# An instruction order from a time model of the engines, and 232 of 4096 exp blocks on VectorE, in a two-layer transformer kernel

## The chip, the cores and the metric

The kernel runs on one core of a Trainium2 chip. The core has TensorE (PE, matrix products into PSUM), ScalarE (ACT, functions of one element such as exp), VectorE (DVE, elementwise work), GpSimd (POOL) and SyncE (SP, which issues DMAs here). Each engine has a queue of its own instructions, in the order in which the program writes them, and waits on semaphores for the others. The metric is the device time of one execution in microseconds; the time given is the median of several runs.

## The reference

```
x = A_x                                     # (1, 2048, 512), bf16
x = x + attention(layernorm(x), wqkv, wo)   # 32 heads of 16 columns
x = x + relu(layernorm(x) @ w1) @ w2        # 512 -> 1792 -> 512
x = x + attention(layernorm(x), wqkv, wo)   # the same weights again
x = x + relu(layernorm(x) @ w1) @ w2

# attention: q, k, v = x @ wqkv, by head
scores = einsum("bhqd,bhkd->bhqk", q, k) * 16 ** -0.5
o      = einsum("bhqk,bhkd->bhqd", softmax(scores), v)
result = o @ wo
```

The scores are 2 layers x 32 heads x 2048 x 2048 numbers, and each goes through an exp.

## The kernel before, in words

Everything stays in SBUF: the weights, the rows `x`, the transposed keys `ktp`, and the values `vaug`, which carry a column of ones beside each head so that the product of probabilities and values also gives the sum of the row. The queries of a layer are cut into four chunks `j` of 512 columns (QS). A *block* is one head, one chunk of 512 queries and one tile of 128 keys (`kb`): one score matmul of 16 used rows (four heads lie in the four row groups of the array) into one PSUM bank of 128 x 512. There are 2 x 4 x 32 x 16 = 4096 blocks.

A *segment* is four heads over the 16 key tiles, 64 blocks. The heads of a group of eight are split in two sets of four by a mask on the queries (`mask[e]`, `qbuf`). Their four P·V products are accumulated in one PSUM bank `ps_o`, each in its own 32 partitions. In the first chunk of layer two, six segments are cut in two runs: the first takes the early key tiles and stores `ps_o` in `acc` ("store"), the second takes the last four key tiles and adds it ("load"), since the last keys of that layer come late.

The main loop takes three blocks (W) at a time, a *slot*. Per slot it writes the score matmuls into one of two PSUM tiles `ps_s` of three banks; then one exp on ScalarE over all 1536 columns into one of four `ebuf` (L628); then the P·V matmuls of the slot before (L545, `emit_pv`); then *pieces* of other work. These pieces are pairs of matmuls of 512 columns, or four transposes, into the one bank `ps_f`: q of the next run, keys, values, output projection, and the two dense products. All of it stands in the lists `urgent` and `work`, and VectorE's part (evacuations of `ps_f`, layer norms, the division by the row sums) in `evac` and `dve_q`. What comes next was chosen by counts of slots: `mark` notes the slot in which a result was written, `ready` asks that it be of an earlier slot, `pace` says how many matmuls of pieces a slot takes, `run_dve(900)` how much of VectorE's list, and `level` counts matmuls. Where `level` falls under FLOOR = 3.4 per slot, the scores are written two or three times (`times`), which changes no result and keeps TensorE occupied.

At the end of a segment (`finish_segment`) VectorE copies `ps_o` to `u`; only then may the next segment's P·V write the bank. Three small DMAs bring the row sums into `c`, bring their reciprocals back to `u`, and spread them over `r`; then VectorE multiplies `u` by `r` into `ot`. After the last segment of a chunk, `rest_of_chunk` puts the projection, layer norms and dense products of that chunk into the list, and they are worked off as pieces of the next chunk.

Of the kernel before, what the change touches and what calls it, by code (L numbers as in the profile page):

```python
# [9 lines left out]
FP32 = mybir.dt.float32  # L10
# [10 lines left out]
def kernel(  # L21
# [34 lines left out]
    FLOOR = 3.4  # L56
# [9 lines left out]
    mask = [sb([P, 1], FP32, f"mask{e}") for e in range(2)]  # L66
    wqkv = sb([P, NDC, 3 * D], BF16, "wqkv")
# [22 lines left out]
    acc = [sb([P, QS], FP32, f"acc{t}") for t in range(NACC)]  # L90
# [53 lines left out]
    slot = [0]  # L144
    made = {}

    def mark(key, lag=0):
        made[key] = slot[0] + lag

    def emitted(deps):  # L150
        return all(k in made for k in deps)

    def ready(deps):
        return all(k in made and (wide[0] or made[k] < slot[0]) for k in deps)
# [5 lines left out]
    dve_q = []  # L160

    def left():
        return sum(c for q in (urgent, work) for g in q for c, _ in g["pieces"]) + sum(
            c for c, _ in cur
        )

    def pick(test):
        for q in (urgent, work):
            for g in q:
                if test(g["deps"]):  # L170
                    q.remove(g)
                    cur.extend(g["pieces"])
                    return True
        return False

    owed = [0.0]

    def run_pe(budget):
        spent = 0.0
        owed[0] = min(owed[0] + budget, 2.0 + budget)  # L180
        while owed[0] > 0:
            if not cur:
                if evac or not pick(ready):
                    break
            c, fn = cur.popleft()
            fn()
            owed[0] -= c
            spent += c
        return spent

    def run_dve(budget):
        i = 0
        while i < len(dve_q) and budget > 0:
            c, deps, fn = dve_q[i]
            if ready(deps):
                dve_q.pop(i)
                fn()
                budget -= c
            else:
                i += 1  # L200

    def run_evac():
        while evac:
            evac.popleft()()

    def force():

        if evac:
            run_evac()
            return True  # L210
        if cur or pick(emitted):
            cur.popleft()[1]()
            return True
        for i, (c, deps, fn) in enumerate(dve_q):
            if emitted(deps):
# [465 lines left out]
```

## Time and profile before

| | |
|---|---|
| median of 3 runs | 2041.85 us (2036.95 to 2048.78) |
| the profiled execution's own time | 2039.66 us |
| its span, first to last instruction | 2037.9 us |
| its mean granted TensorE clock | 0.971 |
| ScalarE busy | 1871.7 us (92%) |
| TensorE busy (matmuls) | 1690.9 us (83%) |
| VectorE busy | 436.9 us (21%) |
| DMA, mean | 14 GB/s |

The profile is of one execution. In its list of groups a row gives line, engine, operation, what is written and read, the form (partitions x elements), how many, the busy time and mean length of one, and the idle time of the engine just before them with what ended it. In the timeline a row gives start and length in us, and in brackets the idle time before it. A busy TensorE is not one at its peak: matmuls overlap, and their ends are modelled. The granted clock is the share of full speed that TensorE's throttle let through.

### The profile page before, as it was taken

What the parts mean: (1) busy time and instruction counts of PE and PEld (TensorE: products, weight loads), DVE (VectorE), ACT (ScalarE), POOL (GpSimd) and SP (SyncE); (2) the same over time, 40 slices, a digit from 0 to 9 for tenths busy, and PEclk for the clock granted to TensorE, in tenths of its full rate; (3) what the DMA queues carried; (4) which work ended last, traced back from release to release, by engine and by line L of the source; (5) the groups of instructions that cost most, each with busy time, mean ns of one, the idle gap of its engine ahead of it and who ended that gap; (6) DMA issues with size and microseconds to landing.
All of it is one profiled execution on the core that took longest, in us unless ns stands there. A gap on an engine that the chain in (4) does not pass through costs nothing.

```text
span 2037.9 us, 30025 instructions
## 1 busy us (share of the span) xinstructions
PE 1690.9 (83%) x13604; PEld 523.4 (26%) x13604; DVE 436.9 (21%) x927; ACT 1871.7 (92%) x1407; POOL 2.4 (0%) x35
## 2 busy tenths in 40 slices
PE   5777778888888888888889877898888888888876
PEld 2222222222222222222222222222222222222222
DVE  5111102212132132212133220211112111121122
ACT  2799999999999999999989999999999999999960
POOL 0000000000000000000000000000000000000000
PEclk8999999999999999999899989989998999989998
DMA  4000000000000000000000010000000000000000
GB/s 155 1 12 12 12 7 12 12 12 6 12 12 11 7 12 12 10 8 12 12 1 1 4 30 9 9 12 12 17 12 12 10 12 19 12 9 10 17 11 11
DMA packets 34131, 29.42 MB, mean 14 GB/s; under 512 B 17492, under 2 KB 25428, under 8 KB 34004
## 3 DMA queue, kind: packets, MB, share of 16 engines
q1 hardware_dynamic: 32420, 25.94, 5.6%
q8 instruction: 106, 1.74, 0.3%
q10 hardware_dynamic: 1584, 1.57, 0.2%
q14 instruction: 21, 0.17, 0.0%
HBM read 7.86 MB, written 2.10 MB: 5 GB/s over the span
## 4 chain that ended last, share of the span: by engine, by line
ACT 71%; PE 17%; DVE 8%; DMA 3%; issue 1%; SPq 0%; DVEq 0%
ACT e L628 71%; PE ps_s L621 6%; PE ps_f L243 5%; PE ps_o L545 4%; DMA r<-u 2%; PE ps_s L243 2%; DVE u L494 1%; DVE ht L400 1%; DVE q L371 1%; PE ps_s L579 1%; DVE stats L260 1%; DMA u<-c 1%; PE ps_f L298 0%; DVE xn L288 0%; ACT xnT L573 0%
## 5 line engine op out<-in xcount | busy, mean ns | idle before, releaser
L628 ACT ACTIVATE e<-ps_s 128x1536 bf16<-128x1536 f32 x1366 | 1847.9, 1581 | 55.1 <-PE ps_s L621 54.2
L621 PE MATMUL ps_s<-q,ktp 32*128 32x512 bf16 x7704 | 812.2, 385 | 221.2 <-ACT e L628 218.8
L545 PE MATMUL ps_o<-e,vaug 128*32 128x512 bf16 x4096 | 568.7, 396 | 45.3 <-DVE u L494 34.6
L621 PEld LDWEIGHTS <-ktp 32*128 32x128 bf16 x7704 | 257.2, 92 | 714.5 <-issue 659.7
L545 PEld LDWEIGHTS <-vaug 128*32 128x32 bf16 x4096 | 138.1, 93 | 490.3 <-issue 490.3
L243 PE MATMUL ps_f<-xn2T,w 128*128 128x512 bf16 x400 | 121.2, 391 | 11.1 <-DVE q L371 5.1
L400 DVE TENSOR_SCALAR ht<-ps_f 128x512 bf16<-128x512 f32 x99 | 68.4, 691 | 281.0 <-PE ps_f L243 281.0
L243 PE MATMUL ps_f<-w,ht 128*128 128x512 bf16 x406 | 120.0, 383 | 1.0
L499 DVE SCALAR_TENSOR_TENSOR ot<-u,mask,r 128x512 bf16<-128x512 f32 (+1 forms) x67 | 48.7, 727 | 276.5 <-DMA r<-u 273.8
L494 DVE COPY u<-ps_o 128x512 f32<-128x512 f32 x58 | 40.1, 691 | 266.5 <-PE ps_o L545 266.5
L243 PE MATMUL ps_f<-xnT,wqkv 128*128 128x512 bf16 x248 | 74.1, 389 | 1.4 <-DVE vaug L363 0.2
L371 DVE TENSOR_SCALAR q<-ps_f,mask 128x512 bf16<-128x512 f32 x68 | 47.9, 746 | 90.2 <-PE ps_f L243 90.2
L243 PE MATMUL ps_f<-wo,ot 128*128 128x512 bf16 x224 | 66.2, 386 | 0.8
L414 DVE TENSOR_TENSOR x<-x,ps_f 128x512 bf16<-128x512 bf16 x29 | 20.0, 688 | 189.2 <-PE ps_f L243 189.2
L386 DVE TENSOR_TENSOR x<-x,ps_f 128x512 bf16<-128x512 bf16 x28 | 19.2, 687 | 161.1 <-PE ps_f L243 161.1
L243 PEld LDWEIGHTS <-w 128*128 128x128 bf16 x448 | 32.0, 99 | 76.4 <-issue 67.5
L260 DVE BATCH_NORM_STATS2 stats<-x 128x6 f32<-128x512 bf16 x64 | 44.0, 687 | 7.0 <-DMA x<-in_A_x_dram 5.6
L338 DVE CAST ktp<-ps_f 128x512 bf16<-128x512 f32 x28 | 19.4, 692 | 117.1 <-PE ps_f L243 117.1
L243 PEld LDWEIGHTS <-ht 128*128 128x128 bf16 x448 | 29.1, 97 | 57.5 <-issue 47.9
L398 ACT ACTIVATE ht<-ps_s 128x512 bf16<-128x512 f32 x6 | 3.6, 597 | 42.8 <-PE ps_s L243 42.8
L298 PE MATMUL ps_f<-ident,xn 128*128 128x128 bf16 x188 | 21.8, 249 | 16.3 <-DVE xn L288 10.0
L298 PEld LDWEIGHTS <-xn 128*128 128x128 bf16 x256 | 18.4, 109 | 54.6 <-DVE xn L288 31.7
(54 smaller groups left out, 303.1 us busy)
## 6 DMA issues: line engine op xcount, KB each, us to landing
r<-u SPq DMA_DIRECT2D x63, 256.0 KB
w<-in_B_w_dram SPq DMA_DIRECT2D x2, 1792.0 KB
x<-in_A_x_dram SPq DMA_DIRECT2D x16, 128.0 KB
out_dram<-x SPq DMA_DIRECT2D x16, 128.0 KB
wqkv<-in_A_wqkv_dram ACTq DMA_DIRECT2D x3, 512.0 KB
c<-u SPq DMA_DIRECT2D x63, 8.0 KB
u<-c SPq DMA_DIRECT2D x63, 8.0 KB
wo<-in_A_wo_dram SPq DMA_DIRECT2D x1, 512.0 KB
```

The lines of the kernel that those rows point to most:

```text
L243: nc.tensor.matmul(b, lhsT, rhs, start=(i == 0), stop=(i == n - 1))
L260: nc.vector.bn_stats(out=st[:], in_=x_t[j * TPC + i][:])
L298: nc.tensor.transpose(pt[:, c * P : (c + 1) * P], xnbuf[i][:, c * P : (c + 1) * P], ident[:])
L371: nc.vector.tensor_scalar(out=qbuf[n % 2][e][:], in0=b, scalar1=mask[e][:, 0:1], scalar2=None, op0=ALU.mult,)
L400: nc.vector.tensor_scalar(out=ht[ft][:], in0=b, scalar1=0.0, scalar2=None, op0=ALU.max)
L414: nc.vector.tensor_add(out=x_t[tt][:], in0=x_t[tt][:], in1=b)
L494: nc.vector.tensor_copy(out=u[:], in_=ps_o[:])
L499: nc.vector.scalar_tensor_tensor(out=ot[t][:, a : a + w], in0=u[:, a : a + w], scalar=mask[e][:, 0:1], in1=r[:, a : a + w], op0=ALU.mult, ...
L545: nc.tensor.matmul(ps_o[32 * g : 32 * g + 32, :], vaug[sg["l"]][kb][:, 4 * sg["T"] + g, 2 * e : 2 * e + 32], s["e"][:, w, :], start=(kb == ...
L579: nc.tensor.matmul(b, lhsT, rhs, start=(i == 0), stop=(i == len(mms) - 1))
L621: nc.tensor.matmul(b[:, w, :], kt[32 * g : 32 * g + 32, kc : kc + P], qbuf[sg["n"] % 2][sg["e"]][32 * g : 32 * g + 32, :], start=True, sto ...
L628: ex = nc.scalar.activation(out=eb[:, :m, :], in_=b[:, :m, :], func=ACTF.Exp, scale=SCALE)
```

## The change

**The order.** The counts of slots give way to clocks, kept while the program is written: `now_pe`, `now_dve` and `exp_end`, in nanoseconds, with a fixed cost for each task, for a hand-over between engines and for a switch of TensorE between kinds of work. `mark` notes an engine and a time, and `at` says when another engine may use the result. `fill_pe` writes pieces ahead of a slot's scores as far as they end before these are needed, `times` is limited by the room that is left, and the floor is 0.56 of the time. `run_dve` takes VectorE's work in three classes: `musts` (the copy of `ps_o`, the first step of a block's exp), then evacuations, then tasks. When a segment ends in a slot, the rest of that slot's P·V is written after the next slot's scores.

**The blocks.** In segments that neither store nor load, a slot may give its third block to VectorE: its exp then covers 1024 columns. Blocks come in pairs, two slots apart. `first_step` adds a bias to the scores, which the mask on the queries (now `qmask`) has scaled so that they read as exponent and fraction of a float, and writes them as whole numbers in `di`. For the two halves together `chain` takes out the fraction (`dm`), runs a cubic polynomial on it in three steps (`dy`, `dy`, `de`), and keeps the exponent in `di`. The probability is the sum of twice `de` and the upper half of `di`, and that sum is formed on TensorE: six P·V matmuls for a pair instead of two. A pair begins where no other is open, not later than the slot 12 of a segment, and where `now_dve` with the tasks that could run is less than 3000 ns ahead of `now_pe`. It comes out as two pairs in each of the 58 segments. `acc` now shares the space of `dm`, `dy` and `di`.

Matmuls in the program: scores 7704 before, 6503 after; P·V 4096 before, 3864 + 464 (`de`) + 232 (`di`) after. The order before the first exp and behind the last keeps its work.

VectorE where chunk 2 of layer two has just been projected, at the end of the first segment of chunk 3 (`ya` ends a layer norm's small operations, `xn` are its four normalizations, `ot` is the multiply by `r`, `q` are the two masked copies of the next queries, `u` is the copy of `ps_o`). Before:

```order
L282 SCALAR_TENSOR_TENSOR ya_199<-ta_201,ya_199 128x4
L499 SCALAR_TENSOR_TENSOR ot_161<-u_183,mask_64,r_185 128x512
L288 TENSOR_SCALAR xn_189<-x_78,mv_195,ya_199 128x512
L288 TENSOR_SCALAR xn_190<-x_79,mv_195,ya_199 128x512
L288 TENSOR_SCALAR xn_191<-x_80,mv_195,ya_199 128x512
L288 TENSOR_SCALAR xn_192<-x_81,mv_195,ya_199 128x512
L371 TENSOR_SCALAR q_0_181<-ps_f,mask_64 128x512
L371 TENSOR_SCALAR q_1_182<-ps_f,mask_65 128x512
L494 COPY u_184<-ps_o 128x512
L323 COPY xn2T<-ps_f 128x4x128 x2
```

The copy of `ps_o` stands behind the multiply, the normalizations and the queries. After:

```order
L386 SCALAR_TENSOR_TENSOR ya_199<-ta_201,ya_199 128x4
L617 COPY u_184<-ps_o 128x512
L707 TENSOR_SCALAR di<-ps_s_205 128x512
L732 TENSOR_SCALAR dm<-di 128x1024
L738 SCALAR_TENSOR_TENSOR dy<-dm 128x1024
L481 TENSOR_SCALAR q_0_181<-ps_f,qmask_66 128x512
L481 TENSOR_SCALAR q_1_182<-ps_f,qmask_67 128x512
L738 SCALAR_TENSOR_TENSOR dy<-dy,dm 128x1024
L738 SCALAR_TENSOR_TENSOR de<-dy,di 128x1024
L732 TENSOR_SCALAR di<-di 128x1024
L392 TENSOR_SCALAR xn_189<-x_80,mv_195,ya_199 128x512
```

The copy comes right behind the layer norm's small operations, then a first step; queries and normalizations stand within and behind the chain.

TensorE at the same segment end (`ps_s` scores, `ps_o<-e` P·V; `vaug_15` and `vaug_0` are the values of the last and the first key tile). Before:

```order
L621 LDWEIGHTS ktp_1_0_105
L621 MATMUL ps_s_204<-q_0_179,ktp_1_0_105 128x512
L545 LDWEIGHTS vaug_15_129
L545 MATMUL ps_o<-e_177,vaug_15_129 32x512
L545 LDWEIGHTS vaug_0_130
L545 MATMUL ps_o<-e_177,vaug_0_130 32x512 [waits DVE_49]
L545 LDWEIGHTS vaug_0_130
L545 MATMUL ps_o<-e_177,vaug_0_130 32x512
L621 LDWEIGHTS ktp_1_0_105
L621 MATMUL ps_s_205<-q_0_179,ktp_1_0_105 128x512 [waits Activation_49]
```

The P·V of the next segment, which waits for VectorE's copy, stands ahead of the scores of the next slot. After:

```order
L668 LDWEIGHTS vaug_15_131
L668 MATMUL ps_o<-e_177,vaug_15_131 32x512
L849 LDWEIGHTS ktp_1_0_107 [waits DVE_49]
L849 MATMUL ps_s_205<-q_0_179,ktp_1_0_107 128x512 [waits Activation_49]
L849 LDWEIGHTS ktp_1_0_107
L849 MATMUL ps_s_205<-q_0_179,ktp_1_0_107 128x512
L849 LDWEIGHTS ktp_1_0_107
L849 MATMUL ps_s_205<-q_0_179,ktp_1_0_107 128x512
L668 LDWEIGHTS vaug_0_132
L668 MATMUL ps_o<-e_177,vaug_0_132 32x512 [waits DVE_49]
```

The scores of the next slot stand ahead of that P·V; they wait for VectorE themselves, for the first step that reads the same tile.

A pair's six matmuls on TensorE, in the second segment of layer two's third chunk; before there are none:

```order
L668 LDWEIGHTS vaug_4_136
L668 MATMUL ps_o<-e_177,vaug_4_136 32x512
L668 LDWEIGHTS vaug_0_132
L668 MATMUL ps_o<-de,vaug_0_132 32x512 [waits DVE_49]
L668 LDWEIGHTS vaug_2_134
L668 MATMUL ps_o<-de,vaug_2_134 32x512
L668 LDWEIGHTS vaug_0_132
L668 MATMUL ps_o<-de,vaug_0_132 32x512
L668 LDWEIGHTS vaug_2_134
L668 MATMUL ps_o<-de,vaug_2_134 32x512
L668 LDWEIGHTS vaug_0_132
L668 MATMUL ps_o<-di,vaug_0_132 32x512 [waits DVE_49]
```

Both halves read `de` twice and the upper half of `di` once (two rows further, for the other half); the first matmul waits for the chain.

The diff, cut:

```
--- before.py
+++ after.py
...
-    FLOOR = 3.4
...
+    KAPPA_BITS = 0x00170000
+    LOG2E = 1.4426950408889634
+    UNIT = float(1 << 23)
+    EXP_BIAS = (126.0 + math.log2(2.0 * LEAD)) * UNIT
...
+    MM = 216.0
+    SWITCH = 105.0
+    PE_TO_DVE, DVE_TO_PE, ACT_TO_PE, PE_TO_ACT = 220.0, 100.0, 240.0, 222.0
+    FLOOR = 0.56
+    LAST_PAIR = 12
+    BACKLOG = 3000.0
...
+    dm = sb([P, 2, QS], FP32, "dm")
+    dy = sb([P, 2, QS], FP32, "dy")
+    di = sb([P, 2, QS], FP32, "di")
+    de = sb([P, 2, QS], BF16, "de")
+    acc = [x[:, k, :] for x in (dm, dy, di) for k in range(2)]
...
+    def at(keys, engine):
+
+        t = 0.0
+        for k in keys:
+            if k not in made:
+                return None
+            e, when = made[k]
+            if e != engine:
+                when += PE_TO_DVE if engine == "dve" else DVE_TO_PE
+            t = max(t, when)
+        return t
...
+    def pe_start(kind, ready=0.0):
+        return max(now_pe[0] + (SWITCH if mode[0] != kind else 0.0), ready)
+
+    def pe_run(kind, units, ready=0.0):
+        now_pe[0] = pe_start(kind, ready) + units * MM
+        mode[0] = kind
+        busy[0] += units * MM
...
+    def fill_pe(limit):
+
         while owed[0] > 0:
+            limit_now = limit if owed[0] < 5.0 else now_pe[0] + 1000.0
...
+                start = pe_start("f", bank_free[0] + DVE_TO_PE) + 50.0
+                for g in (g for q in (urgent, work) for g in q):
+                    t = at(g["deps"], "pe")
+                    if t is not None and t <= start:
+                        break
+                else:
+                    return
+                if start + g["pieces"][0][0] * MM > limit_now:
+                    return
+                start_group(g)
+            elif pe_start("f", cur[0][2]) + cur[0][0] * MM > limit_now:
+                return
+            do_piece()
...
+    def run_dve(until, musts):
+
+        while True:
+            can = [(0, m[1], m) for m in musts[:1]]
+            if now_dve[0] < until:
+                can += [(1, e[1], None) for e in list(evac)[:1]]
+                for t in dve_q:
+                    ready = at(t["deps"], "dve")
+                    if ready is not None:
+                        can.append((2, ready, t))
+            if not can:
+                return
+            soon = [c for c in can if c[1] <= now_dve[0] + 40.0]
+            kind, ready, x = min(soon, key=lambda c: c[0]) if soon else min(can, key=lambda c: c[1])
+            if kind and ready >= until:
+                if not musts:
+                    return
+                kind, ready, x = can[0]
+            if kind == 0:
+                musts.pop(0)
+                dve_run(x[0], x[1])
+                x[2]()
+            elif kind == 1:
+                do_evac()
             else:
-                i += 1
-
-    def run_evac():
+                do_task(x)
...
+        def masked(b, e):
+            nc.vector.tensor_scalar(
+                out=qbuf[n % 2][e][:], in0=b, scalar1=qmask[e][:, 0:1], scalar2=None,
+                op0=ALU.mult,
+            )
+
         def fin(b):
-            for e in range(2):
-                nc.vector.tensor_scalar(
-                    out=qbuf[n % 2][e][:], in0=b, scalar1=mask[e][:, 0:1], scalar2=None,
-                    op0=ALU.mult,
-                )
-            mark(("q", n))
+            masked(b, 0)
...
+        if n > 1:
+            run_until(("m", n - 2))
...
+                mark(("c", n), lag=2600.0)
...
+            mark(("r", n), lag=5500.0)
...
+    def dve_block(half, sg, kb, g, src, ex, recent):
+        def first_step():
+            first = nc.vector.tensor_scalar(
+                out=di[:, half, :].bitcast(I32), in0=src, scalar1=EXP_BIAS, scalar2=0.0,
+                op0=ALU.add, op1=ALU.max,
+            )
+            tc.declare_no_dep(
+                first.ins, ex.ins, reason="both only read the scores, and in different banks"
+            )
+            for earlier in recent:
+                tc.declare_no_dep(
+                    first.ins, earlier,
+                    reason="the scores read here were written after it, and are waited for",
+                )
+            step1_end[slot[0]] = now_dve[0]
+            if half == 1:
+                chain(pairs[-1]["key"])
+
+        if half == 0:
+            assert not pairs
+            pair_no[0] += 1
+            pairs.append({"sg": sg, "key": ("e", pair_no[0]), "blocks": []})
+        pairs[-1]["blocks"].append((kb, g))
+        musts.append((690, now_pe[0] + PE_TO_DVE, first_step))
...
+    def chain(key):
+        def bits(out, keep, put):
+            nc.vector.tensor_scalar(
+                out=out[:].bitcast(I32), in0=di[:].bitcast(I32), scalar1=keep,
+                scalar2=put, op0=ALU.bitwise_and, op1=ALU.bitwise_or,
+            )
+
+        def step(out, x, c, y):
+            nc.vector.scalar_tensor_tensor(
+                out=out[:], in0=x[:], scalar=c, in1=y[:], op0=ALU.add, op1=ALU.mult
+            )
+
+        steps = (
+            (690, lambda: bits(dm, 0x007FFFFF, 0x3E800000)),
+            (1260, lambda: step(dy, dm, C2, dm)),
+            (1260, lambda: step(dy, dy, C1, dm)),
+            (1260, lambda: step(de, dy, C0, di)),
+            (690, lambda: bits(di, 0x7F800000, KAPPA_BITS)),
+        )
+        for n, (cost, fn) in enumerate(steps):
+            k = key + (n,) if n + 1 < len(steps) else key
+            task(cost, fn, [k], [key + (n - 1,)] if n else [], place=n)
+
+    def emit_pair():
+        p = pairs.popleft()
+        pe_run("v", 3, at([p["key"]], "pe"))
+        halves = list(enumerate(p["blocks"]))
+        tops = di[:].bitcast(BF16)
+        for rhs in (de, de, None):
+            for half, (kb, g) in halves:
+                pv(p["sg"], kb, g, tops[:, half, 1::2] if rhs is None else rhs[:, half, :])
 
 
...
+        pace = 3.0 if sg["store"] or sg["load"] else max(todo / max(rest - 6.0, 6.0), 0.5)
+        owed[0] = min(owed[0] + pace, 6.0) if todo else 0.0
+        s_ready = max(exp_end[no - 2] + ACT_TO_PE, step1_end.get(no - 2, 0.0) + DVE_TO_PE)
+        need_by = exp_end[no - 1] - MM - PE_TO_ACT
+        fill_pe(max(need_by - 60.0, s_ready) - SWITCH)
+
...
+        spare = int(max(need_by - pe_start("s", s_ready), 0.0) / MM)
+        times = 1 + min(spare, 0 if level >= 0 else 1 if level > -MM else 2)
...
+        half = None
+        if len(now) == W and now[0][0] is sg and not (sg["load"] or sg["store"]):
+            r = (kb * 4 + g - 2) // W
+            if pair_at is not None:
+                half = 1 if r == pair_at + 2 else None
+            elif (
+                not pairs
+                and r <= LAST_PAIR
+                and now_dve[0] + sum(t["cost"] for t in dve_q if at(t["deps"], "dve") is not None)
+                < now_pe[0] + BACKLOG
+            ):
+                half = 0
+        if half is not None:
+            pair_at = r if half == 0 else None
+        m = len(now) - (half is not None)
+        ex = nc.scalar.activation(
+            out=eb[:, :m, :], in_=b[:, :m, :], func=ACTF.Exp,
+            scale=1.0 / (LOG2E * UNIT),
...
+        copies = len(musts)
+        while len(pend) > 1 and len(musts) == copies:
             emit_pv()
...
+            and (at([pairs[0]["key"]], "pe") or 1e18) <= now_pe[0] + 60.0
+            and all(x[0] is pairs[0]["sg"] for x in list(pend[0]["blocks"])[:1])
+        ):
+            emit_pair()
...
+        level = min(level + busy[0] - FLOOR * (exp_end[no] - exp_end[no - 1]), 90.0)
+        run_dve(exp_end[no - 1] + ACT_TO_PE, musts)
```

More of the change, by code (lines that the diff above doesn't have):

```diff
@@ L1 @@
+import math
 from contextlib import ExitStack
@@ L533, with pv @@
     pend = deque()
-    last_exp = [None] * NE
+    musts = []
+    exps = [deque(maxlen=6) for _ in range(NE)]
+    def pv(sg, kb, g, rhs, stop=False):
+        e = sg["e"]
+        nc.tensor.matmul(
+            ps_o[32 * g : 32 * g + 32, :],
+            vaug[sg["l"]][kb][:, 4 * sg["T"] + g, 2 * e : 2 * e + 32],
+            rhs, start=g not in sg["begun"], stop=stop,
+            tile_position=(0, 32 * g), skip_group_check=True,
+        )
+        sg["begun"].add(g)
     def emit_pv():
@@ L568 @@
                     op=ALU.add, axis=mybir.AxisListType.XY,
+                )
+            for e in range(2):
+                nc.vector.tensor_scalar(
+                    out=qmask[e][:], in0=mask[e][:], scalar1=SCALE * LOG2E * UNIT, scalar2=None,
+                    op0=ALU.mult,
                 )
```

290 lines of the change are left out of this document (174 added, 116 removed).

## The prediction

> **What bounds the kernel now.** I read the page first, its busy shares, the chain that ended last and the costliest groups:
>
> ```profile
> PE 1690.9 (83%) x13604; PEld 523.4 (26%) x13604; DVE 436.9 (21%) x927; ACT 1871.7 (92%) x1407; POOL 2.4 (0%) x35
> ...
> ACT 71%; PE 17%; DVE 8%; DMA 3%; issue 1%; SPq 0%; DVEq 0%
> ...
> L628 ACT ACTIVATE e<-ps_s 128x1536 bf16<-128x1536 f32 x1366 | 1847.9, 1581 | 55.1 <-PE ps_s L621 54.2
> L621 PE MATMUL ps_s<-q,ktp 32*128 32x512 bf16 x7704 | 812.2, 385 | 221.2 <-ACT e L628 218.8
> L545 PE MATMUL ps_o<-e,vaug 128*32 128x512 bf16 x4096 | 568.7, 396 | 45.3 <-DVE u L494 34.6
> ```
>
> ScalarE's exp (L628) is the limit: 1847.9 us of work, with only 55.1 us idle before it. The score matmuls wait 218.8 us for exp; exp waits 54.2 us for them. TensorE looks 83% busy, but the score row counts 7704 matmuls for 4096 blocks: the rest repeat scores to keep TensorE occupied. VectorE is idle four fifths of the time.
>
> Next, ScalarE's timeline, for the price of an exp, and the query on the exp's line:
>
> ```profile
> 128.49 86.24 ACT L628 ACTIVATE e<-ps_s 128x1536 bf16<-128x1536 f32 x64 [0.37 <-PE ps_s L621]
> ...
> 358.83 1.45 ACT L628 ACTIVATE e<-ps_s 128x1536 bf16<-128x1536 f32 x1 [0.60 <-PE ps_s L621]
> ...
> L628 ACT ACTIVATE e<-ps_s x1366: 602/1557/1802, 67.4 to 1969.8; 128x1536 bf16<-128x1536 f32 x195, 128x512 bf16<-128x512 f32 x1
> ```
>
> Alone, an exp of three blocks takes 1.45 us. In a train of 64 the pitch is (86.24 - 1.45) / 63 = 1.346 us, so two neighbours overlap by 0.104. The shortest, 602 ns, is the one exp of a single block that ends the queue of blocks. Exps run from 67.4 to 1970; what lies before and after (67 and 68 us) the diff leaves in its order.
>
> Third, the waits of ScalarE, for the whole run and for five stretches (67 to 965, 965 to 1207, and three of 17 to 20 us at 1320, 1555 and 1795):
>
> ```profile
> ACT e L628 <- PE ps_s L621: 54.2, 109, 2.4
> ...
> ACT e L628 <- PE ps_s L621: 13.8, 28, 1.3
> ...
> ACT e L628 <- PE ps_s L621: 23.0, 43, 2.1
> ...
> ACT e L628 <- PE ps_s L621: 2.7, 7, 0.6
> ...
> ACT e L628 <- PE ps_s L621: 4.0, 8, 1.5
> ...
> ACT e L628 <- PE ps_s L621: 4.3, 8, 2.4
> ```
>
> The 23.0 lie in the runs that store and load `acc`, where matmul pieces are pushed at pace 3.0; 11.0 in the three short stretches. The last of these, in the timeline and by windows:
>
> ```profile
> 1790.97 0.16 DVE L282 SCALAR_TENSOR_TENSOR ya<-ta,ya 128x4 f32<-128x4 f32 x1
> 1791.06 0.75 DVE L499 SCALAR_TENSOR_TENSOR ot<-u,mask,r 128x512 bf16<-128x512 f32 x1
> ...
> 1791.73 1.38 DVE L288 TENSOR_SCALAR xn<-x,mv,ya 128x512 bf16<-128x512 bf16 x4
> ...
> 1793.02 1.41 DVE L371 TENSOR_SCALAR q<-ps_f,mask 128x512 bf16<-128x512 f32 x2
> ...
> 1794.34 0.69 DVE L494 COPY u<-ps_o 128x512 f32<-128x512 f32 x1
> ...
> 1795.08 0.61 PE L545 MATMUL ps_o<-e,vaug 128*32 128x512 bf16 x2 [2.25 <-DVE u L494]
> ...
> 1797.14 1.45 ACT L628 ACTIVATE e<-ps_s 128x1536 bf16<-128x1536 f32 x1 [2.39 <-PE ps_s L621]
> ...
> 1809.18 18.91 ACT L628 ACTIVATE e<-ps_s 128x1536 bf16<-128x1536 f32 x14 [0.21 <-PE ps_s L621]
> ...
> 1797.00:1806.00 9.00, 9.00 (x58) 2.72 (x55) 1.86 (x5) 7.67 (x6) 0.00 (x0) 0.50 0.09 18
> ```
>
> At the end of a segment the copy of `ps_o` stands on VectorE behind a multiply, four normalizations and two q copies. TensorE, in order, waits 2.25 us for it, exp waits 2.39 us, and after this gap the granted clock (last but two columns of the window) is 0.50. Seven exps then take 12.04 us, 1.72 each.
>
> **The change, part by part.**
>
> *232 blocks leave ScalarE.* The order of the changed program holds 1366 exps still, 232 of them of 1024 columns. Between 0.602 for one block and 1.45 for three, a block costs 0.424 us, so an exp of two has a pitch of 0.922: 232 x 0.424 = 98 us less. At most it is a third of the pitch, 0.449 (104 us); at least 0.32 (74 us), if the shorter exp lost the overlap of 0.104. I take 98, since an exp of two lies between two measured sizes and stands in the same train.
>
> *VectorE takes them.* Rows for its durations:
>
> ```profile
> L494 DVE COPY u<-ps_o 128x512 f32<-128x512 f32 x58 | 40.1, 691 | 266.5 <-PE ps_o L545 266.5
> ...
> L499 DVE SCALAR_TENSOR_TENSOR ot<-u,mask,r x67: 352/752/754, 109.7 to 1977.3; 128x512 bf16<-128x512 f32 x63, 128x128 bf16<-128x128 f32 x4
> ...
> L278 DVE SCALAR_TENSOR_TENSOR ta<-ya 128x4 f32<-128x4 f32 x48 | 7.8, 162 | 1.6
> ```
>
> The first step (L707) reads one PSUM bank as the `u` copy does: 232 x 0.69 = 160 us. Three two-tensor steps per pair have 1024 columns: between 0.752 + 0.59 = 1.34 (752 less the 162 of a four-column one, once more) and twice 0.752; at 1.34 they are 348 x 1.34 = 466. The two steps on bits read SBUF alone, and no row has their form: four normalizations of 512 columns took 1.38, so 0.69 per 1024 at that rate, or 1.38 at the `u` copy's; 160 or 320 us. VectorE so goes from 437 to about 1220 us (at the upper ends 1440), 63% to 75% of 1930. It does not become the bound by sum. A pair's chain lasts 5.4 us (upper ends 7.3).
>
> *New wait: scores behind the first step.* Scores of exp n+2 overwrite the bank that the first step of exp n reads, and the order shows that wait on their first weight load, with everything on TensorE queued behind. Score rows and their waits:
>
> ```profile
> 200.00 0.61 PE L621 MATMUL ps_s<-q,ktp 32*128 32x512 bf16 x6 [0.19 <-ACT e L628]
> ...
> 700.13 0.39 PE L621 MATMUL ps_s<-q,ktp 32*128 32x512 bf16 x3
> ...
> 700.45 0.40 PE L545 MATMUL ps_o<-e,vaug 128*32 128x512 bf16 x3
> ...
> 701.31 0.10 PEld L621 LDWEIGHTS <-ktp 32*128 32x128 bf16 x3 [0.42 <-issue]
> ```
>
> Scores n end about 0.6 us after exp n-2 ends; exp n then ends 1.346 + 0.922 after that point, 1.65 later. A first step with nothing before it on VectorE ends 0.9 after the scores (0.69 and a hand-over of about 0.2, as the 0.19 above), and the scores have some 0.55 to spare within the next exp (1.346 less 0.39 and two hand-overs). It may be 1.3 us late for nothing: about one two-tensor step in front of it. Only behind two operations, or behind a layer norm's twelve small ones (2.4 us), does it show. Bounds: 0 and 232 x 0.69 = 160 us; I take one step in ten late by 0.5 us, 12 us, near the lower end because copies and first steps go ahead of other VectorE work in the new order.
>
> *New wait: a pair's six matmuls behind its chain.* By the changed order five or six exps pass between a pair's second first step and its matmuls, 6.7 to 8.1 us at 1.346, against 5.4 of chain: 0 taken; the rival below has the price.
>
> *TensorE.* Score matmuls fall from 7704 to 6503, P·V rise from 4096 to 3864 + 464 + 232 = 4560. Three matmuls cost 0.32 with the switch (700.13 to 700.45). All 13604 - 737 = 12867 in 1930 us are 6.67 per us, as now (13604 in 2038). Work beside the exp; 0 taken. The longest slot, scores, P·V and a piece of two, took 1.18 us (700.13 to 701.31), which fits beside an exp of three but not of two; only four exps in 21 are short, so pieces move to others.
>
> *The order at segment ends.* TensorE now has the next scores ahead of the P·V that waits for the copy, and VectorE takes the copy before multiply, normalizations and q copies (both places above). The layer norm's twelve small operations still stand ahead of it, so of the 11.0 us I take 8 away; of the 20 us at other segment ends (54.2 - 23.0 - 11.0) 14; of the 23.0 nothing, since the pace there stays. Together 22; bounds 0 and 54.
>
> *The multiply that waits for a DMA.*
>
> ```profile
> 215.60 0.25 DVE L517 RECIPROCAL c<-c 128x16 f32<-128x16 f32 x1
> 224.48 0.75 DVE L499 SCALAR_TENSOR_TENSOR ot<-u,mask,r 128x512 bf16<-128x512 f32 x1 [8.63 <-DMA r<-u]
> ```
>
> `r` lands 8.6 us after the reciprocal; the new table reckons with 5.5. A multiply put 5.5 behind would block VectorE for 3.1. In the new order two first steps and a chain (6.8 us) with other work stand between nearly everywhere; 0 taken, 58 x (3.1 - 1.3) = 104 at worst. SP's queue issues the same transfers; a few output stores move up by one place.
>
> The sum, against the profiled execution's own 2039.7 us (2.2 below the median of the three runs, span 2037.9): 2039.7 - 98 - 22 + 12 = 1932 us.
>
> **The rivals.** *Late chains.* If the bit steps run at 1.38 and the two-tensor steps at 1.50, a chain lasts 7.3 us; with the two q copies that often stand in it (1.41) it ends 8.7 after the first step, 1.3 behind the mean of 7.4 that the order leaves. TensorE waits, 0.55 of it is spare, 116 x 0.75 = 87 us come back: about 2020, or 1975 for half of it. For it: no row has the bit form, and VectorE's queue is in order. Against it: the normalization row. [...]
>
> *Slower: the clock.* TensorE's clock falls to half after a gap, and an exp then takes 1.72 us, where the mean of the changed kernel's would be (1134 x 1.346 + 232 x 0.922) / 1366 = 1.27. It decides from (108 + 10) / 0.45 = 262 exps, 450 us more at half clock, a mean granted clock below about 0.87; at 300 exps the time is 1932 + 135 = 2067. For it: 1201 repeated scores fewer, and VectorE, busier, can hold TensorE for 2 us. Against it: the same matmuls per us, and in 2038 us few gaps were long enough. [...] This trace has it after a gap of 2.25, so the measurement keeps this rival alive.
>
> *No change that can be told* (within 0.5%, 10 us, about what a measurement of this kernel can tell): the waits eat the whole 98 us, late chains at full price and half the DMA's.
>
> **How the numbers follow.** The forecast, 1892 to 1970, 0.64: its lower end has 104 instead of 98, another 32 us of idle gone and no late step (2039.7 - 104 - 44). Late chains, 1970 to 2031: 0.21. Below 1892: 0.03. No change: 0.05. Slower by the clock: 0.07. Faster by over 0.5% is 0.64 + 0.21 + 0.03 = 0.88. The range 1892 to 2000 leaves out 0.03 below and about 0.17 above.
>
> **What would show it.** Exp busy near 1750 us with idle before it at 30 to 45; VectorE busy 1200 to 1250, bit steps at 0.69 and two-tensor steps at 1.34; little waiting of `ps_s` matmuls for `di` and of `ps_o` for `de` (each below 30 us); mean clock of 0.96 or more; no 2 us gap at 1790's place. Wrong it would be if the pitch of a 1024-column exp is far from 0.922, if first steps or chains hold TensorE for over 60 us, or if the clock falls.

## The result and the profile after

The changed kernel takes 1900.12 us (median of 4 runs, 1895.87 to 1904.3), the kernel before 2041.61 on the same chip: ratio 0.9304, 95% interval 0.9268 to 0.934. Forecast were 1932, range 1892 to 2000: the direction and the range held, and the gain, 142 us, was a third more than the 108 forecast. The profiled execution took 1897.81 us, its span 1896.0.

The page of the changed kernel, the lines that answer to those of before:

```profile
PE 1654.1 (87%) x12867; PEld 520.5 (27%) x12867; DVE 1149.9 (61%) x1741; ACT 1764.1 (93%) x1407; POOL 2.4 (0%) x35
...
ACT 83%; PE 8%; DVE 4%; DMA 3%; issue 1%; SPq 0%; DVEq 0%
...
L870 ACT ACTIVATE e<-ps_s 128x1536 bf16<-128x1536 f32 (+1 forms) x1366 | 1740.3, 1589 | 20.9 <-PE ps_s L849 19.8
L849 PE MATMUL ps_s<-q,ktp 32*128 32x512 bf16 x6503 | 720.3, 385 | 171.5 <-ACT e L870 135.7
L707 DVE TENSOR_SCALAR di<-ps_s 128x512 int32<-128x512 f32 x232 | 159.7, 688 | 319.8 <-PE ps_s L849 319.1
L738 DVE SCALAR_TENSOR_TENSOR dy<-dm 128x1024 f32<-128x1024 f32 x116 | 142.1, 1225 | 3.7
L738 DVE SCALAR_TENSOR_TENSOR de<-dy,di 128x1024 bf16<-128x1024 f32 x116 | 141.8, 1223 | 2.9
L732 DVE TENSOR_SCALAR dm<-di 128x1024 int32<-128x1024 int32 x116 | 80.3, 692 | 3.5
```

ScalarE is still the limit, and more of the chain that ended last runs through it (83%, 71% before). Exp is busy 107.6 us less (1847.9 to 1740.3) and idle 34.2 less (55.1 to 20.9): together 141.8, the change of the span (2037.9 - 1896.0 = 141.9). VectorE, at 61%, has room. Its own steps came in at 0.688, 0.692 and 1.22 us.

All of exp's waits for scores, and the new waits on VectorE, in the changed kernel (total us, times, longest):

```profile
PEld L849 <- DVE dm L732: 27.9, 67, 0.8
...
ACT e L870 <- PE ps_s L849: 19.8, 27, 2.5
PEld L849 <- DVE di L707: 10.2, 18, 3.1
PE ps_o L668 <- DVE u L617: 7.2, 11, 2.2
...
PE ps_s L849 <- DVE di L707: 5.5, 2, 2.8
```

Exp waits 27 times, 109 times before. TensorE's score matmuls and their weight loads wait 43.6 us for VectorE in the rows with `dm` and `di`, mostly about 0.4 us at a time; exp itself waits 19.8 us, so most of it is covered. For `de` no P·V matmul waits.

The segment end that the prediction showed at 1790, in the timeline of the changed kernel:

```profile
1668.52 0.16 DVE L386 SCALAR_TENSOR_TENSOR ya<-ta,ya 128x4 f32<-128x4 f32 x1
1668.60 0.68 DVE L617 COPY u<-ps_o 128x512 f32<-128x512 f32 x1
1669.20 0.68 DVE L707 TENSOR_SCALAR di<-ps_s 128x512 int32<-128x512 f32 x1
...
1669.34 0.40 PE L668 MATMUL ps_o<-e,vaug 128*32 128x512 bf16 x4 [1.60 <-DVE u L617]
...
1670.26 1.45 ACT L870 ACTIVATE e<-ps_s 128x1536 bf16<-128x1536 f32 x1 [0.71 <-PE ps_s L849]
```

The copy still comes behind the layer norm's small operations and TensorE still waits 1.60 us for it, but scores of the next slot went ahead: exp waits 0.71, where it waited 2.39. Behind the 1.60 us TensorE's granted clock still falls, to 0.50 from 1670 to 1673.

### The profile page after: what moved, and what is told of

It reads as the page before. It is cut to its first block, busy times and chain, and to the rows that moved or that the text cites. A ratio compares the mean times of both kernels' runs of the same rounds, so it can differ in the third digit from the quotient of the medians.

```text
span 1896.0 us, 29515 instructions
## 1 busy us (share of the span) xinstructions
PE 1654.1 (87%) x12867; PEld 520.5 (27%) x12867; DVE 1149.9 (61%) x1741; ACT 1764.1 (93%) x1407; POOL 2.4 (0%) x35
## 4 chain that ended last, share of the span: by engine, by line
ACT 83%; PE 8%; DVE 4%; DMA 3%; issue 1%; SPq 0%; DVEq 0%
ACT e L870 83%; PE ps_s L849 2%; DMA r<-u 2%; PE ps_f L347 2%; PE ps_s L347 2%; PE ps_o L668 1%; PE ps_s L789 1%; DMA u<-c 1%; DVE stats L364 1%; ACT xnT L783 0%; PE ps_s L401 0%; DVE ot L628 0%; DMA x<-in_A_x_dram 0%; DVE q L481 0%; DVE ktp L446 0%
## 5 line engine op out<-in xcount | busy, mean ns | idle before, releaser
L870 ACT ACTIVATE e<-ps_s 128x1536 bf16<-128x1536 f32 (+1 forms) x1366 | 1740.3, 1589 | 20.9 <-PE ps_s L849 19.8
L849 PE MATMUL ps_s<-q,ktp 32*128 32x512 bf16 x6503 | 720.3, 385 | 171.5 <-ACT e L870 135.7
L707 DVE TENSOR_SCALAR di<-ps_s 128x512 int32<-128x512 f32 x232 | 159.7, 688 | 319.8 <-PE ps_s L849 319.1
L738 DVE SCALAR_TENSOR_TENSOR dy<-dm 128x1024 f32<-128x1024 f32 x116 | 142.1, 1225 | 3.7
L738 DVE SCALAR_TENSOR_TENSOR de<-dy,di 128x1024 bf16<-128x1024 f32 x116 | 141.8, 1223 | 2.9
L738 DVE SCALAR_TENSOR_TENSOR dy<-dy,dm 128x1024 f32<-128x1024 f32 x116 | 141.7, 1221 | 2.6
L732 DVE TENSOR_SCALAR dm<-di 128x1024 int32<-128x1024 int32 x116 | 80.3, 692 | 3.5
L732 DVE TENSOR_SCALAR di<-di 128x1024 int32<-128x1024 int32 x116 | 80.3, 692 | 3.2
L668 PE MATMUL ps_o<-de,vaug 128*32 128x512 bf16 x464 | 79.3, 382 | 0.0
L628 DVE SCALAR_TENSOR_TENSOR ot<-u,mask,r 128x512 bf16<-128x512 f32 (+1 forms) x67 | 48.4, 722 | 36.1 <-DMA r<-u 33.4
L668 PE MATMUL ps_o<-di,vaug 128*32 128x512 bf16 x232 | 54.7, 391 | 0.0
```

What stands on the lines that cost most here:

```text
L628: nc.vector.scalar_tensor_tensor(out=ot[t][:, a : a + w], in0=u[:, a : a + w], scalar=mask[e][:, 0:1], in1=r[:, a : a + w], op0=ALU.mult, ...
L668: nc.tensor.matmul(ps_o[32 * g : 32 * g + 32, :], vaug[sg["l"]][kb][:, 4 * sg["T"] + g, 2 * e : 2 * e + 32], rhs, start=g not in sg["begun ...
L707: first = nc.vector.tensor_scalar(out=di[:, half, :].bitcast(I32), in0=src, scalar1=EXP_BIAS, scalar2=0.0, op0=ALU.add, op1=ALU.max,)
L732: nc.vector.tensor_scalar(out=out[:].bitcast(I32), in0=di[:].bitcast(I32), scalar1=keep, scalar2=put, op0=ALU.bitwise_and, op1=ALU.bitwise_or,
L738: nc.vector.scalar_tensor_tensor(out=out[:], in0=x[:], scalar=c, in1=y[:], op0=ALU.add, op1=ALU.mult)
L849: nc.tensor.matmul(b[:, w, :], kt[32 * g : 32 * g + 32, kc : kc + P], qbuf[sg["n"] % 2][sg["e"]][32 * g : 32 * g + 32, :], start=True, sto ...
```

## The experiments

Three accounts of the 142 us had to be told apart: the new order is worth more than the 22 taken for it; a block that leaves ScalarE is worth more than 0.424; or TensorE's clock did it. The last two columns are of the profiled execution; time at half clock is 2 x (1 - mean clock) x span, which takes the clock as full or half (in windows of 1 us of the kernel before it is 1.00 in 1906, 0.50 in 107 and between them in 24). Differences between runs are taken from the ratios, times 2041.6, since the kernels did not all run on one chip. Of the twelve expectations below, e1, e2, e3, e4, e6, e8 and e9 came out outside every range that they name, and e7 between two; e1b, e2b, e4b and e10 fell into one.

| run | median us | ratio to before, 95% | exp busy / idle us | half clock us |
|---|---|---|---|---|
| before | 2041.61 | 1 | 1847.9 / 55.1 | 118 |
| after | 1900.12 | 0.9268 to 0.934 | 1740.3 / 20.9 | 91 |
| e1_order_only | 2018.13 | 0.9777 to 0.9934 | 1842.9 / 41.0 | 182 |
| e2_blocks_free | 1934.97 | 0.9393 to 0.9499 | 1749.9 / 51.9 | 282 |
| e1b_order_floor | 1996.82 | 0.9743 to 0.981 | 1837.2 / 24.4 | 84 |
| e2b_free_floor | 1892.78 | 0.9241 to 0.9306 | 1738.5 / 14.9 | 79 |
| e9_floor | 1909.95 | 0.9313 to 0.9356 | 1742.2 / 31.6 | 115 |
| e3_old_segment_end | 1912.93 | 0.9305 to 0.9395 | 1745.2 / 27.8 | 99 |
| e8_before_pv_later | 2015.49 | 0.9826 to 0.9899 | 1843.7 / 33.9 | 117 |
| e4_long_chain | 2073.77 | 1.0088 to 1.0182 | 1758.5 / 172.6 | 252 |
| e4b_long_chain_told | 1918.31 | 0.9362 to 0.9427 | 1748.4 / 33.1 | 115 |
| e7_r_lag | 1894.22 | 0.9243 to 0.9303 | 1739.8 / 20.7 | 102 |
| e6_no_repeats | 1934.47 | 0.9419 to 0.9474 | 1749.1 / 55.7 | 458 |
| e10_best | 1939.75 | 0.9455 to 0.9514 | 1728.2 / 69.7 | 120 |

**The order alone, the blocks alone.** In the first, no slot gives a block away; in the second, slots give them and the model counts the cost, but VectorE's steps and the pairs' matmuls are not issued.

```
e1:   -    LAST_PAIR = 12
      +    LAST_PAIR = -1
e2:   first_step's instruction left out; in chain:
      -            task(cost, fn, ...)
      +            task(cost, lambda: None, ...)
      in emit_pair:
      -                pv(p["sg"], kb, g, ...)
      +                pass
```

> The new order alone: no pair is ever begun, so all 4096 blocks stay on ScalarE. Theory A (the two parts add up): the blocks are worth their 98 us and the order the rest of the 142 us that the span fell by, so this comes to about 1998 us (1985 to 2010), with exp busy near 1840 us, idle before the exps near 20 us, and about 30 idle gaps instead of 109. Rival B (the order pays only because shorter exps and fewer repeated scores leave room): within 10 us of before, 2030 to 2050, idle before exps still 45 us or more.

> The changed kernel with VectorE's part of the 232 blocks left out: no first step, no chain, none of a pair's six matmuls; everything else stands where it did, and the exps of two blocks stay. It leaves out those blocks' probabilities. Theory A: VectorE's 745 us and the 696 matmuls are hidden, so at most the idle before the exps (20.9 us) and the overlap lost at its gaps (3 us) can go: 1880 to 1897 us. Rival B (waits on VectorE hold TensorE and cost more than ScalarE's idle shows): 1870 us or less.

Neither split the sum: e2 does less than the changed kernel and takes 29 us more (0.9446 against 0.9304). With 182 and 282 us of half clock both stand far above the 91 of the changed kernel. Where it began in e1, in windows (us, then busy time of PE, PEld, DVE, ACT and POOL with instructions, granted clock, DMA share, GB/s):

```profile
180.00:245.00 65.00, 50.22 (x456) 16.05 (x456) 9.63 (x17) 65.00 (x49) 0.00 (x0) 1.00 0.05 10
...
249.00:300.00 51.00, 51.00 (x309) 9.24 (x309) 2.45 (x4) 43.78 (x31) 0.00 (x0) 0.50 0.04 9
```

and in its timeline, the last score groups before and the first within:

```profile
246.83 0.83 PE L849 MATMUL ps_s<-q,ktp 32*128 32x512 bf16 x9 [0.62 <-ACT e L870]
...
248.18 0.81 PE L849 MATMUL ps_s<-q,ktp 32*128 32x512 bf16 x6 [0.19 <-ACT e L870]
...
249.52 1.04 PE L849 MATMUL ps_s<-q,ktp 32*128 32x512 bf16 x6
```

The clock halves at about 249 and stays there for 60 us with no gap over 0.62 us in the 24 us before it, and exp falls from 49 in 65 us to 31 in 51. In those 51 us TensorE wrote 216 score matmuls, where 31 exps need 93: at half clock the repeats fill it. So both were run again with more repeated scores.

**The same with FLOOR at 0.64.**

```
-    FLOOR = 0.56
+    FLOOR = 0.64
```

> The new order alone, with the floor of TensorE's time raised from 0.56 to 0.64 (8148 score matmuls instead of 7569; repeats change no result). In the run at 0.56 the clock halved for 61 us from 250 us on, without a gap on TensorE. If that and other half clock is what kept it 20 us over theory A, the clock stays up here and it comes to 1990 to 2003 us with under 130 us of half clock. If the order alone simply is worth less (rival B), or the repeats get in the way of scores: 2010 us or more.

> VectorE's part of the 232 blocks left out as in the run before (their probabilities are missing), with the floor raised from 0.56 to 0.64. If that run was slower than the changed kernel only because TensorE, with 696 matmuls fewer, fell under what keeps its clock, this one comes to 1880 to 1897 us with under 110 us of half clock, and VectorE's work with its waits then costs the changed kernel 0 to 18 us. If something else was slow in it: 1915 us or more.

The same stretch in e1b:

```profile
180.00:245.00 65.00, 54.68 (x515) 17.45 (x522) 9.15 (x16) 65.00 (x50) 0.00 (x0) 1.00 0.05 10
249.00:300.00 51.00, 43.33 (x443) 15.06 (x441) 2.95 (x5) 51.00 (x39) 0.00 (x0) 1.00 0.05 10
```

The clock holds, and with 84 and 79 us of half clock the two compare. Their exps, in e1b and then in e2b:

```profile
L870 ACT ACTIVATE e<-ps_s 128x1536 bf16<-128x1536 f32 x1366 | 1837.2, 1695 | 24.4 <-PE ps_s L849 24.2
```

```profile
L858 ACT ACTIVATE e<-ps_s 128x1536 bf16<-128x1536 f32 (+1 forms) x1366 | 1738.5, 1556 | 14.9 <-PE ps_s L837 14.5
```

Order alone: ratio 0.9777, 2041.6 x 0.0223 = 45 us less. In its profile that is 30.7 of idle and 10.7 of busy time, of 42.0 in the span. At the changed kernel's own floor, in e1, the order is worth 30 us (0.9855; 13 to 46 by the interval), with twice that kernel's half clock. Blocks off ScalarE: 0.9777 to 0.9273, 103 us; exp busy falls by 98.7, and 98.7 / 232 = 0.425 us a block, the 0.424 taken.

**VectorE's part at that floor.** The changed kernel with FLOOR 0.64 differs from e2b by the work that e2b leaves out.

> The changed kernel with the floor at 0.64 instead of 0.56 (7263 score matmuls instead of 6503). If half clock within the main loop (some 44 us in the changed kernel's profile) comes partly from low occupation: 1886 to 1896 us. If it comes from gaps alone, which the floor does not close: 1896 to 1904. With VectorE's part left out the same floor gave 1892.8 us, so the difference of the two is what VectorE's part costs: 0 to 10 us.

From 0.9273 to 0.9335: 12.7 us for first steps, chains and pairs, with exp idle 14.9 to 31.6. The two intervals leave about 8 us either way, and 3 to 6 of the 12.7 may be the clock (79 and 115 us of half clock, at the prices below). Against the changed kernel (0.9304) e9 is not told apart; that kernel itself is 6 us above e2b. At one floor the three terms run 45 + 103 - 13 = 135 us, against 2041.6 x 0.0665 = 136 by e9's own ratio. They must agree, since each difference begins where the one before ends; this is no test of the parts. The third account, the clock, is small: 27 us less half clock than before (118 to 91) are 2 to 5 us at those prices.

**The order at segment ends.** e3 takes it out of the changed kernel; e8 puts it alone into the kernel before, so that a slot's P·V behind a segment's end is written after the next scores.

```
e3:  -        copies = len(musts)
     -        while len(pend) > 1 and len(musts) == copies:
     +        while len(pend) > 1:
                  emit_pv()
     +            run_dve(0.0, musts)
e8 (before; finish_segment sets ended[0]):
     -        while len(pend) > 1:
     +        ended[0] = False
     +        while len(pend) > 1 and not ended[0]:
                  emit_pv()
```

> The changed kernel, but at a segment's end the copy of ps_o and the rest of the slot's P.V are written at once, ahead of the next slot's scores, as before. Theory A: of the 34 us of idle that went, the gaps at segment ends return, 40 to 60 of 0.3 to 0.6 us, with the overlap of 0.1 each: 1915 to 1935 us. Rival B (VectorE's priority for the copy did it, not TensorE's order): 1895 to 1905 us.

> The kernel before with one part of the new order: when a segment ends in a slot, the rest of that slot's P.V is written after the next slot's scores (VectorE's order, the counts of slots and all blocks on ScalarE as before). Undoing this part in the changed kernel cost 13 us. If it stands for itself: the gaps at segment ends, 20 us before, shrink, and the time is 2018 to 2032 us. If it needs VectorE's new order (the copy first): within 8 us of before.

In the changed kernel it is worth 0.46% (0.935 against 0.9304, 9 us), within the intervals; the wait of P·V for the copy shows the edit, in e3 and then in e8:

```profile
PE ps_o L668 <- DVE u L617: 31.0, 41, 1.3
...
ACT e L870 <- PE ps_s L849: 25.2, 44, 3.5
```

```profile
ACT e L630 <- PE ps_s L623: 33.3, 76, 1.7
...
PE ps_o L547 <- DVE u L494: 4.3, 3, 2.3
```

Alone in the old order it gives 1.4% (0.9863), 28 us: exp's idle time falls from 55.1 to 33.9 and the wait for the copy from 34.6 (row of before: `ps_o` 45.3, of it 34.6) to 4.3. Within the new order fewer gaps are left for it, 44 in e3 against 109 in the kernel before, and the other part of the order takes mostly the same waits. In the stretch of the runs that store and load `acc` (windows of equal ends, as explained further below; 894.8 to 1128 in e3, 959.8 to 1195.3 in e8), exp waits 23.0 us in 43 gaps before, 12.4 in 34 in e8, 11.3 in 16 in e3 and 9.4 in 12 in the changed kernel; outside it 31.2, 20.9, 13.9 and 10.4. So the two parts do not add up.

**Late chains.** Two of the chain's five steps are done twice, so that VectorE has 1.9 us more in each pair: in e4 the model is not told, in e4b it is.

```
e4:   -            (690, lambda: bits(dm, ...)),
      -            (1260, lambda: step(dy, dm, C2, dm)),
      +            (690, lambda: (bits(dm, ...), bits(dm, ...))),
      +            (1260, lambda: (step(dy, dm, C2, dm), step(dy, dm, C2, dm))),
e4b:  the same with 1380 and 2490 for 690 and 1260
```

> The changed kernel with the first bit step and the first two-tensor step of each chain done twice (the same result is written again), and the model not told: a chain lasts 5.06 + 0.69 + 1.23 = 7.0 us, the length of the rival of late chains. By that rival's price TensorE waits at most pairs and 50 to 87 us come back: 1950 to 1985 us. Theory A (the order leaves enough cover, VectorE at 73% is no bound): under 15 us, 1895 to 1915 us.

> The long chain again (two of five steps done twice), but with the model told their double cost; it then makes 220 blocks on VectorE. Capacity theory (VectorE at 70% is too busy whatever the order): 2030 us or more, as untold. Lateness theory (the order was written for a shorter chain, and what it put behind came late: evacuations of ps_f, first steps, pairs): 1900 to 1925 us, 12 blocks of 0.424 us and some idle above the changed kernel.

Untold, the kernel is slower than the one before (1.0135): 170 us more than the changed kernel. Told, it costs 18, with 220 blocks in place of 232. VectorE is at 66% in the one and 69% in the other (1370.5 and 1318.3 us busy), so it is lateness that costs, and hardly load. Of the 170, some 13 to 27 us may be the clock, by 161 us more half clock at the prices below. Where e4 waits:

```profile
ACT e L870 <- PE ps_s L849: 169.8, 174, 3.7
PE ps_f L347 <- DVE ht L514: 36.7, 25, 2.0
...
PE ps_o L668 <- DVE de L738: 26.0, 42, 1.1
PE ps_f L347 <- DVE x L528: 20.2, 15, 2.5
...
PE ps_f L347 <- DVE x L499: 14.9, 9, 1.9
```

The pairs' own matmuls wait 26.0 us. Matmuls of pieces wait 71.8 in these three rows for evacuations of `ps_f` that stand behind the longer chain on VectorE, with the scores behind them on TensorE; in the changed kernel the same three rows come to 0.5.

**The multiply that waits for `r`.** The model's 5.5 us between reciprocal and `r` become the measured 8.6.

```
-            mark(("r", n), lag=5500.0)
+            mark(("r", n), lag=8600.0)
```

> The changed kernel with the one number of the table that the trace contradicts put right: r is reckoned 8.6 us after the reciprocal instead of 5.5. In the changed kernel six multiplies hold VectorE for 33.4 us in all, and exp's gaps of 1.80 us at 465 and 2.55 us at 1122 end behind two of them, each with 10 us of half clock after it. If these are what is left: 1885 to 1894 us, exp idle under 16 us. If the waits are hidden anyway: 1896 to 1904 us, no change.

In the changed kernel, and below it in e7:

```profile
DVE ot L628 <- DMA r<-u: 33.4, 6, 8.6
```

```profile
DVE ot L628 <- DMA r<-u: 8.6, 1, 8.6
```

Most of the wait goes, exp's idle time stays (20.9 to 20.7), and the ratio 0.9273 (0.9243 to 0.9303) is not told apart from 0.9304. The gap at 1122 has 3.4 us of half clock behind it in the windows, not the 10 that the expectation gives.

**No repeated scores.** FLOOR at 0 leaves 4096 score matmuls.

> The changed kernel with the floor at 0: no scores are repeated (4096 score matmuls instead of 6503; the results are the same). If the clock follows how busy TensorE is, as the two runs without pairs suggest, it is at half for most of the run; at half clock scores and P.V take about 0.55 us each and a piece of two 1.0, so TensorE becomes the bound: 2000 us or more, mean clock under 0.8. If only gaps of 2 us close it: 1890 to 1915 us with a clock of 0.96 or more.

```profile
249.00:300.00 51.00, 42.25 (x255) 11.56 (x252) 24.47 (x31) 49.77 (x40) 0.00 (x0) 0.69 0.06 11
```

The mean clock falls to 0.882, yet the kernel loses only 29 us (0.9447 against 0.9304): exp still does 40 in 51 us at a clock of 0.69 (42 in the changed kernel).

**More blocks.** Pairs one slot apart, up to the last slot, with more backlog, `lag` 8600 and FLOOR 0.64: 284 blocks.

```
-    FLOOR = 0.56
-    LAST_PAIR = 12
-    BACKLOG = 3000.0
+    FLOOR = 0.64
+    LAST_PAIR = 16
+    BACKLOG = 6000.0
-                half = 1 if r == pair_at + 2 else None
+                half = 1 if r == pair_at + 1 else None
```

> A version meant to be faster: the two blocks of a pair in neighbouring slots instead of two apart, the last start at slot 16 and a backlog of 6000 ns, which makes 284 blocks on VectorE instead of 232; r reckoned at 8.6 us; the floor at 0.64. If blocks go on at 0.424 us each: 52 x 0.424 = 22 us under the changed kernel, and up to 6 from the two numbers: 1870 to 1880 us. If pairs now end too late in their segments and hold TensorE, or VectorE at 70% comes late as in the long chain that the model was not told of: 1900 us or more.

Slower than the changed kernel by 37 us. Exp is busy 12.1 us less and idle 48.8 more; its waits:

```profile
ACT e L870 <- PE ps_s L849: 66.1, 88, 3.8
...
PE ps_o L668 <- DVE u L617: 19.8, 51, 0.9
PE ps_o L668 <- DVE de L738: 18.3, 9, 2.6
```

Here late chains do come, at 68% of VectorE: P·V waits 18.3 us for `de`. Several numbers were changed at once, and their shares in the 37 us were not separated. No run with all of the work in it beats the changed kernel by more than the intervals.

## Why the prediction was right, and which term was mis-sized

*What bounds the kernel:* right. In every run the change in exp's busy and idle time is that of the span within about 2 us.

*232 blocks, 98 us:* right; e1b and e2b give 98.7 in exp's busy time. An exp of two alone, in the timeline of the changed kernel, lies between the two sizes as taken (0.602 + 0.424 = 1.026):

```profile
477.28 1.02 ACT L870 ACTIVATE e<-ps_s 128x1024 bf16<-128x1024 f32 x1 [1.45 <-PE ps_s L849]
```

*VectorE:* 1149.9 us busy, under the 1200 to 1250 expected, and 73 under the sum of 1223: two-tensor steps took 1.22 and not 1.34 (348 x 0.12 = 42 us), and the other 31 are overlaps, since the rows of VectorE's groups sum to 41 over its busy time, against 10 before. Steps on bits took 0.69, not 1.38. This decided the rival of late chains: a chain has 2 x 0.69 + 1.225 + 1.221 + 1.223 = 5.1 us and is not late. On the same 1024 columns a step on bits took 692 ns and the two-tensor step `de` 1223, 1.77 times as long.

*Late first steps, 12 us:* 12.7 by e9 against e2b, but this is luck in part: it holds chains, pairs' matmuls and clock as well, has about 8 either way, and is 6 if the changed kernel is set against e2b. TensorE's waits for VectorE at the scores, 43.6 us with the rows named `dm`, are above the 30 I had set, and most of it is covered.

*The order, 22 us: this term failed, by half.* e1b has 45, in its profile 41.4 of exp's time: 14.1 of idle time in the stretch below, 15.9 outside it, 8.7 of overlap (84 gaps fewer) and 2.7 over. I had taken 0, 22 and 0. So two steps in it were wrong, both put at nothing. The first is "of the 23.0 nothing, since the pace there stays". The runs that store and load `acc`, in windows that begin and end at the same distance from the first copy to `acc` and the last sum with it (before 965 to 1207, after 896.5 to 1125), before and then after:

```profile
965.00:1207.00 242.00, 209.22 (x1545) 61.82 (x1543) 66.42 (x133) 218.76 (x159) 0.00 (x0) 0.94 0.04 8
```

```profile
896.50:1125.00 228.50, 204.92 (x1469) 61.41 (x1463) 89.71 (x170) 218.52 (x164) 0.00 (x0) 0.94 0.04 9
```

```profile
ACT e L870 <- PE ps_s L849: 9.4, 12, 2.5
```

The same busy ScalarE (218.8 and 218.5) in 13.5 us less; the last row is its wait there now, 23.0 in 43 before. In e1b, with all blocks on ScalarE (949.7 to 1180), that row is

```profile
ACT e L870 <- PE ps_s L849: 8.9, 13, 1.7
```

so the blocks are not the reason. The pace stays, but where pieces stand in a slot is now chosen by the clock of the model. This is what e3 keeps and e8 does not have, and most of the small gaps go with it (16 left in e3, 34 in e8); the order at segment ends, which these runs have too, shortens the wait there by itself as well (12.4 in e8). These are exps of the stretch in ScalarE's timeline, before and then after.

```profile
1060.39 1.45 ACT L628 ACTIVATE e<-ps_s 128x1536 bf16<-128x1536 f32 x1 [1.84 <-PE ps_s L621]
1062.20 4.16 ACT L628 ACTIVATE e<-ps_s 128x1536 bf16<-128x1536 f32 x3 [0.36 <-PE ps_s L621]
1066.57 1.45 ACT L628 ACTIVATE e<-ps_s 128x1536 bf16<-128x1536 f32 x1 [0.20 <-PE ps_s L621]
```

```profile
956.78 114.43 ACT L870 ACTIVATE e<-ps_s 128x1536 bf16<-128x1536 f32 x85 [0.40 <-PE ps_s L849]
```

A train that broke off after every three or four exps now runs over 85. The second wrong step is in the price of a gap: I took its idle time alone, but each gap also loses the overlap of 0.104 of its two neighbours. 82 gaps fewer (109 to 27) are 8.5 us, and that stands in the busy time: 107.6 = 98.4 + 8.5, and 0.7 over. Idle time outside the stretch fell by 31.2 - 10.4 = 20.8, after the late first steps; with these at 12 the forecast had a net of 10. So the 34 us that the forecast missed are 13.6 in the stretch, 8.5 of overlap and about 11 at other places. These 11 are not more order: without blocks, in e1b, the idle time outside fell by 15.9, less than the 22 taken. They match the 12 taken for late first steps, which this kernel's idle time does not show; e9, which differs by the floor alone, has 10.7 us more of it, so what one arrangement of repeats gives by chance is of that size.

*The DMA, 0:* right within the noise. The multiply still waits for `r` six times, 33.4 us in all and at most 8.6, and e7 moved the time by less than its interval.

*The clock:* it does fall behind a gap (to 0.50 behind 1.60 us at 1669), but its price was set too high. By the rival, 450 us at half clock would cost over 118. e6 has 367 more than the changed kernel and lost 29, 0.08 per us; e1 against e1b 16 for 98 (0.0078 of 2041.6), 0.16; e2 against e2b 35 for 203 (0.0173), 0.17; 0.26 was assumed (0.45 of 1.72). That was too high in itself: 1.72 was measured on exps of three blocks, at a pitch of 1.346 otherwise, and was set against a mean of 1.27 that has shorter exps in it. The three prices are estimates: each pair of runs differs in its repeats as well, and the intervals of e1 and e1b overlap. e6 has 117 score matmuls for 40 exps in its window and e1 216 for 31, so repeats written at half clock are a likely reason why e1 pays more; no run takes them apart.

*Late chains:* the rival did not come to pass, but was priced at 87 us, for P·V alone; e4 shows 170, with more of the waiting at `ps_f` than at P·V.

*Sums that do not come out:* with another 32 us of idle gone the lower end would be 1932 - 6 - 32 - 12 = 1882, and the 44 in its sum is 10 short. For no change, late chains at 87 need about 21 of the DMA's 104 to make up 108, not half. At 1900 us the result is inside the range either way.

## What to carry to other kernels

On the engine that sets the time, count the gaps as well as their length: a gap costs its idle time and the overlap of two neighbours (0.104 us here), and an order by modelled clocks can take out many small ones that no single wait announces. In a static order a task's true duration belongs in the model: the same longer chain cost 18 us told and 170 untold. When leaving work out to price it, look at the granted clock first; here less work on TensorE made a slower kernel (e2, by 29 us at a mean clock of 0.927 against 0.976).

## What was not expected of the hardware

TensorE's clock halved in e1 at 249 us with no gap of over 0.62 us in the 24 us before, and stayed there for 60 us with TensorE busy nearly all the time at that rate (51.00 of 51.00 us from 249 to 300). In the changed kernel it fell to 0.50 behind a gap of 1.60 us at 1669. A count of matmuls hardly explains it: e1 had 456 in the 65 us before, and e4 kept the full clock with 457 (463 by its weight loads) and TensorE busy 52.56 us against 50.22 in the same window:

```profile
180.00:245.00 65.00, 52.56 (x457) 17.10 (x463) 49.86 (x60) 63.83 (x51) 0.00 (x0) 1.00 0.05 10
```

What sets it stays open. The second thing: with ScalarE as the limit, half the clock of TensorE cost an estimated 0.08 (e6) to 0.17 us per us (e2), and a kernel with 458 us of it (e6) is 1.5% slower than the changed kernel.
